# A fused sparse attention and FFN kernel: all engine orders from a list schedule, and the value product turned around

## Chip, cores and metric

One core of a Trainium2 chip. The metric is the device time of one execution in microseconds; lower is better. A profiled execution gives the span from the first to the last instruction, about 2 us shorter than the time. The profile names TensorE PE (its weight loads PEld), VectorE DVE, ScalarE ACT, GpSimd POOL and SyncE SP.

## The reference

```python
# q, k, v: (4, 8, 768, 64); sampled_blocks: (24, 3), blocks of 32
scores = q @ k.T / 8
mask = |block_i - block_j| <= 1, or first/last block row or column, or sampled
attn = softmax(where(mask, scores, -1e9));  x = attn @ v
x = x.transpose(0, 2, 1, 3).reshape(3072, 512)
out = (((x @ w1) * (x @ w2)) @ w3) @ w_out       # d_ff = 1024
```

Both kernels compute every score, take the exponential without a maximum, multiply by a 0/1 mask, and fold w3 @ w_out into one matrix first.

## The kernel before

The order on each engine is the order of the program text. A step makes two score tiles (`scores`), the values of the step before (`values`), and takes two pieces of weight or FFN work from a queue as filler (`pop`).

```python
def scores(b, t, Q, kp, i):
    s = ps_s.tile([128, 2, 512], F32, ...)                 # 2 buffers, 2 PSUM banks each
    for k2 in range(2):
        for h in range(2):                                 # two heads on the two row halves
            matmul(s[:, h, k2*256:(k2+1)*256], lhsT=kT[64*h:64*h+64, ...128 keys],
                   rhs=qT[64*h:64*h+64, ...256 queries])
    e = Exp(s / 8);  e = e * mask                          # ACT, then DVE
def values(b, t, Q, kp):                                   # output: features x tokens
    for k2 in range(2):
        for part in range(3):
            for g in range(4):                             # four heads on the four column quarters
                if part == 2: matmul(d[32*g:32*g+32], lhsT=ones, rhs=e)          # denominator
                else:         matmul(o[32*g:32*g+32, part], lhsT=v[..32 features], rhs=e)
def normalize(b, t, Q):
    ln = Ln(d);  rec = Exp(-ln)                            # ACT
    x[...] = o * rec                                       # DVE
...
transposes(0, 0); transposes(0, 1)
for t in range(NT): build_mask(t)                          # all masks before the first score
for s, g in enumerate(groups):
    scores(b, t, Q, kp, 0); scores(b, t, Q, kp, 1)
    if prev is not None: values(*prev); finish(prev)
    ...                                                    # transposes of the next batch
    pop(0 if s < 3 else 2)
    prev = g
```

## Time and profile before

| | before |
|---|---|
| time, median (range), first measurement | 300.67 us (299.7 to 305.25) |
| span of the profiled run | 298.6 us |
| busy PE / DVE / ACT | 272.0 / 194.2 / 189.5 us |
| first score, first value | 20.5, 23.7 us |
| granted TensorE clock, mean | 0.997 |

"Busy" counts a matmul from its start to its modelled end, so neighbours overlap and a busy TensorE can still lose time between pieces. The prediction shows how the pace is read from starts. The mean clock leaves out the start: the views give 1.00 there, though the eight score matmuls at 20.52 us take 1.04 us, against 0.61 later, which is half the pace.

### The profile page before, as it was taken

To read this page: it belongs to the slowest core of one execution; us is meant where nothing else is said; L and a number is where in the kernel's file an instruction comes from. 1 tells how busy PE (TensorE), PEld (TensorE's weight loads), DVE (VectorE), ACT (ScalarE), POOL (GpSimd) and SP (SyncE) were. 2 spreads that over 40 slices of the span, in tenths; PEclk is the share of its full clock that TensorE was granted. 3 is DMA by queue.
4 is the path that set the end of the run, shared out by engine and by line. 5 is a ranking of instruction groups with operands and counts; after the bars stand their busy time and mean duration, and the time that the engine had idled before them with its cause. 6 is when DMAs were issued, how large, how long until landed. Compare 5 with 4: busy or idle time off the path is not lost.

```text
span 298.6 us, 7850 instructions
## 1 busy us (share of the span) xinstructions
PE 272.0 (91%) x3412; PEld 141.2 (47%) x3412; DVE 194.2 (65%) x308; ACT 189.5 (63%) x250; POOL 49.6 (17%) x81
## 2 busy tenths in 40 slices
PE   0479888987999999999999999999999999999994
PEld 0335455555454455555455455555445445444441
DVE  3616787778767776776777677677767676643332
ACT  1088766656688886576867887657988778721310
POOL 8634487222200000332100000000000000000000
PEclk9999999999999999999999999999999999999998
DMA  7999999973420002757311000011000120003003
GB/s 96 150 204 207 206 173 186 180 106 55 66 44 2 0 2 108 131 69 106 55 37 73 35 2 2 2 72 70 3 2 1 52 93 2 0 2 140 0 12 129
DMA packets 20053, 21.46 MB, mean 72 GB/s; under 512 B 1588, under 2 KB 14900, under 8 KB 20020
## 3 DMA queue, kind: packets, MB, share of 16 engines
q0 software_dynamic: 16528, 14.68, 32.5%
q1 hardware_dynamic: 3492, 6.29, 5.6%
q8 instruction: 26, 0.43, 0.6%
q14 instruction: 7, 0.06, 0.1%
HBM read 29.36 MB, written 6.29 MB: 119 GB/s over the span
## 4 chain that ended last, share of the span: by engine, by line
PE 68%; ACT 15%; DVE 10%; issue 4%; POOL 1%; ACTq 0%; POOLq 0%
PE o L231 13%; PE pa L290 12%; PE pb L301 12%; ACT e L206 10%; PE po L311 10%; PE s L201 9%; PE wp L272 5%; DVE x L247 4%; PE d L228 4%; ACT rec L246 3%; PE tp L187 3%; DVE qkt L190 2%; ACT ln L244 2%; DVE e L207 1%; ACT mask L177 1%
## 5 line engine op out<-in xcount | busy, mean ns | idle before, releaser
L206 ACT ACTIVATE e<-s 128x1024 bf16<-128x1024 f32 x144 | 139.5, 1021 | 54.8 <-PE s L201 54.4
L207 DVE TENSOR_TENSOR e<-e,mask 128x1024 bf16<-128x1024 bf16 x144 | 99.1, 691 | 55.3 <-ACT e L206 55.3
L231 PE MATMUL o<-e,vn 128*32 128x256 bf16 x1152 | 54.8, 278 | 3.8 <-DVE x L247 1.8
L201 PE MATMUL s<-qkt 64*128 64x256 bf16 x576 | 47.5, 277 | 5.6 <-DVE qkt L190 3.9
L290 PE MATMUL pa<-x,w_sb 128*128 128x512 bf16 x192 | 49.7, 381 | 0.0
L301 PE MATMUL pb<-x,w_sb 128*128 128x512 bf16 x192 | 49.2, 379 | 0.0
L303 DVE TENSOR_TENSOR h<-pb,a 128x512 bf16<-128x512 f32 x48 | 33.1, 690 | 21.2 <-PE pb L301 21.2
L311 PE MATMUL po<-wf_sb,h 128*128 128x512 bf16 x192 | 44.5, 380 | 0.0
L293 ACT CAST a<-pa 128x512 bf16<-128x512 f32 x48 | 28.0, 583 | 26.1 <-PE pa L290 25.7
L228 PE MATMUL d<-e,ones 128*32 128x256 bf16 x576 | 42.4, 276 | 0.0
L201 PEld LDWEIGHTS <-qkt 64*128 64x128 bf16 x576 | 22.8, 95 | 37.5 <-issue 34.8
L231 PEld LDWEIGHTS <-vn 128*32 128x32 bf16 x1152 | 26.9, 96 | 20.5 <-issue 18.4
L301 PEld LDWEIGHTS <-w_sb 128*128 128x128 bf16 x192 | 18.7, 98 | 24.1 <-issue 2.6
L311 PEld LDWEIGHTS <-h 128*128 128x128 bf16 x192 | 17.5, 98 | 21.9 <-issue 2.7
L290 PEld LDWEIGHTS <-w_sb 128*128 128x128 bf16 x192 | 15.7, 98 | 21.1 <-issue 7.0
L316 DVE COPY ob<-po 128x512 f32<-128x512 f32 x24 | 16.5, 688 | 10.2 <-PE po L311 10.2
L85 POOL DMA_DIRECT2D qn<-in_q_dram x16 | 11.7, 728 | 66.7 <-PE tp L187 59.4
L247 DVE TENSOR_TENSOR x<-o,rec 128x512 bf16<-128x512 f32 x24 | 16.6, 692 | 1.6 <-ACT rec L246 0.9
L228 PEld LDWEIGHTS <-ones 128*32 128x32 bf16 x576 | 17.0, 98 | 0.4
L190 DVE COPY qkt<-tp 128x1536 bf16<-128x1536 bf16 x16 | 15.2, 950 | 1.3 <-PE tp L187 1.3
L272 PE MATMUL wp<-wo_sb,w3t_sb 128*128 128x512 bf16 x64 | 15.2, 380 | 0.0
L85 POOL DMA_DIRECT2D vn<-in_v_dram x16 | 11.6, 726 | 17.5 <-PE d L228 14.6
(54 smaller groups left out, 125.7 us busy)
## 6 DMA issues: line engine op xcount, KB each, us to landing
out_dram<-ob SPq DMA_DIRECT2D x24, 256.0 KB, 2.0
qn<-in_q_dram POOLq DMA_DIRECT2D x16, 192.0 KB, 4.2
kn<-in_k_dram POOLq DMA_DIRECT2D x16, 192.0 KB, 4.8
vn<-in_v_dram POOLq DMA_DIRECT2D x16, 192.0 KB, 5.8
w_sb<-in_moe_w_dram POOLq DMA_DIRECT2D x8, 256.0 KB, 10.6
w_sb<-in_moe_w_dram POOLq DMA_DIRECT2D x16, 128.0 KB, 5.3
wo_sb<-in_moe_w_out_dram POOLq DMA_DIRECT2D x1, 1024.0 KB, 11.3
rand_sb<-in_sampled_blocks_dram SPq DMA_DIRECT2D x1, 0.6 KB
```

The costliest lines, as they stand in the source:

```text
L201: nc.tensor.matmul(s[:, h, k2 * QT:(k2 + 1) * QT], lhsT=qk[64 * h:64 * h + 64, 1, kc * 128:(kc + 1) * 128], rhs=qk[64 * h:64 * h + 64, 0, ...
L206: nc.scalar.activation(e, s, AF.Exp, scale=1.0 / 8.0)
L207: nc.vector.tensor_tensor(e, e, mask[:, t, kp:kp + 1, :].to_broadcast((128, 2, 512)), op=ALU.mult)
L228: nc.tensor.matmul(d[rows, :], lhsT=ones, rhs=rhs, start=first, stop=last, skip_group_check=True)
L231: nc.tensor.matmul(o[rows, part * QT:(part + 1) * QT], lhsT=vn[b, 2 * Q + i][:, h, kc, 32 * part:32 * part + 32], rhs=rhs, start=first and ...
L247: nc.vector.tensor_tensor(X[i][:, 2 * Q:2 * Q + 2, half * QT:(half + 1) * QT], o.rearrange("p (s n) -> p s n", s=2), rec.to_broadcast((128 ...
L272: nc.tensor.matmul(box["p"], lhsT=w3t_sb[:, j, i * 128:(i + 1) * 128], rhs=wo_sb[:, j, :], start=j == 0, stop=j == NF - 1)
L290: nc.tensor.matmul(p, lhsT=w1_sb[:, c, f * 128:(f + 1) * 128], rhs=x[:, c, :], start=c == 0, stop=c == 3)
L293: nc.scalar.copy(a, p)
L301: nc.tensor.matmul(p, lhsT=w2_sb[:, c, f * 128:(f + 1) * 128], rhs=x[:, c, :], start=c == 0, stop=c == 3)
L303: nc.vector.tensor_tensor(hT[:, f, :], p, box["a"], op=ALU.mult)
L311: nc.tensor.matmul(box["o"], lhsT=hT[:, f, n * 128:(n + 1) * 128], rhs=wf_sb[:, f, :], start=f == 0, stop=f == NF - 1)
```

## The change

Intent: the number of TensorE columns falls, and so does the number of changes of array shape (from the full array to row halves or column quarters, and back). Every engine's order comes from a list schedule, a program that gives each free engine a ready task in turn; it runs at build time over a table of durations, buffers and a model of the DMA rings (the queues of transfers), instead of from the program text. The core:

```diff
+        for j, ...:                                       # tokens x features, full array
+            for k2 in range(2):
+                for qt in range(2):
+                    for h in range(2):
+                        nc.tensor.matmul(o[:, qt, h, :], lhsT=e[:, j, h, lo:lo + 128],
+                                         rhs=w[:, h, kc, :], ...)     # [v, 1]: 65 columns
+        rec = reciprocal(o[:, :, :, 64:]);  xn = o[:, :, :, :64] * rec          # DVE
+        nc.sync.dma_start(out=x[...], in_=xn[:, qt, :], transpose=True)         # 24 of them
-                        nc.tensor.matmul(d[rows, :], lhsT=ones, rhs=rhs, ...)
-                        nc.tensor.matmul(o[rows, ...], lhsT=vn[..., 32 columns], rhs=rhs, ...)
-        nc.scalar.activation(ln, d, AF.Ln);  nc.scalar.activation(rec, ln, AF.Exp, scale=-1.0)
-        nc.vector.tensor_tensor(e, e, mask)               # 144 of 1024 elements
+        nc.vector.tensor_tensor(e, e, mask)               # 72 of 2048 elements
+    # first q/k pair in halves by SP and ACT queues, cast on chip; 20 of 32 q/k and 2 of 8 w3
+    # transposes by DMA; w1, w2 in natural row order; 59 dummy matmuls on zeros at the start
+class Task:  # costs per engine, deps, buffers written and read, priority, array shape
+class Rings: # two DMA queues sharing the engines packet by packet; gives each landing time
+class Plan:
+    def run(self):
+        while ...:
+            # for each ready task: earliest start from deps (+ 0.05 to 0.195 us to be seen),
+            # free buffers and the engine; the earliest pick of all engines is committed
+    def pick_pe(self, cands, free, mode):
+        # stay in the score shape while scores are ready; enter it when both score buffers
+        # are (nearly) free; otherwise by priority
+log = plan.run()
+for t in log: t.go(t)                                     # the program text in that order
```

## The prediction

> **What bounds the kernel now.** I read the page's engine shares and 40 slices first, then the groups, then the timeline of a steady stretch, of the start and of the end. The time is 300.67 us, the profiled span 298.6 us, so I count in the span and take the time as up to 1% more.
>
> The page, engine shares and two rows of the slices:
>
> ```profile
> PE 272.0 (91%) x3412; PEld 141.2 (47%) x3412; DVE 194.2 (65%) x308; ACT 189.5 (63%) x250; POOL 49.6 (17%) x81
> ...
> PE   0479888987999999999999999999999999999994
> ...
> DMA  7999999973420002757311000011000120003003
> ```
>
> TensorE is the bound: after the first tenth it is nearly always busy, DVE and ACT are at two thirds. But busy is not peak, so I need its real pace. A steady step of the timeline (columns: start, duration, engine, line, operation):
>
> ```profile
> 146.40 0.61 PE L201 MATMUL s<-qkt 64*128 64x256 bf16 x8
> 146.83 1.94 ACT L206 ACTIVATE e<-s 128x1024 bf16<-128x1024 f32 x2 [0.61 <-PE s L201]
> 146.94 0.40 PE L231 MATMUL o<-e,vn 128*32 128x256 bf16 x8
> ...
> 147.71 1.04 PE L290 MATMUL pa<-x,w_sb 128*128 128x512 bf16 x4
> ...
> 148.58 1.03 PE L301 MATMUL pb<-x,w_sb 128*128 128x512 bf16 x4
> ...
> 149.54 0.61 PE L201 MATMUL s<-qkt 64*128 64x256 bf16 x8
> ```
>
> One step (two score tiles, their values, eight FFN matmuls) takes 149.54 - 146.40 = 3.14 us: scores 0.54, values and denominators 0.77, FFN 0.87 + 0.96. ACT works 1.94 us of exponentials and waits, so ACT is not the limit. Two more rows give the pace of back-to-back matmuls, the first from 285 us on, the second from 53 us on:
>
> ```profile
> 287.46 7.07 PE L311 MATMUL po<-wf_sb,h 128*128 128x512 bf16 x32
> ...
> 55.17 0.62 PE L259 MATMUL w3p<-ident,w_sb 128*128 128x128 bf16 x8
> ```
>
> With one matmul's own 0.38 and 0.22 us taken off, a 512-column matmul takes (7.07 - 0.38)/31 = 0.216 us, a 128-column one with its weight load (0.62 - 0.22)/7 = 0.057 us. The line through both is 0.0045 us + 0.000413 us per column: estimates of 0.110 us for 256 columns and 0.031 us for 65. The step then has 4 x 0.110 (score matmuls run in pairs of row halves) + 6 x 0.110 (values in fours of column quarters) + 8 x 0.216 = 2.83 us of streaming; the other 0.31 us lies at its three changes of array shape, about 0.10 us each. Over the kernel:
>
> - streaming: scores 31.7 (288 slots), values with denominators 47.5 (432 slots), FFN 124.4 (576), weight fold 13.8 (64), q/k transposes 11.0 (192 slots), w3 transposes 3.7, masks 2.3; sum 234.4 us
> - shape changes in 72 steps: 72 x 0.31 = 22.3 us
> - the start: scores begin at 20.5 us with about 3.8 us of TensorE work before them, so 16.7 us are lost
> - the end: last matmul at about 294.5 us, then copy and store, 4.1 us
> - the rest, 298.6 - 277.5 = 21.1 us: transposes wedged into 16 steps, half-speed matmuls and waits for exponentials around 20 to 30 us, single waits, and the FFN tail
>
> The start and end:
>
> ```profile
> 10.60 0.59 PE L167 MATMUL gp<-hot,Ab 24*24 24x512 bf16 x1 [10.60 <-DVE Ab L161]
> ...
> 12.26 0.85 PE L187 MATMUL tp<-ident,qn 128*64 128x128 bf16 x12
> ...
> 20.52 1.04 PE L201 MATMUL s<-qkt 64*128 64x256 bf16 x8
> ...
> 294.56 0.69 DVE L316 COPY ob<-po 128x512 f32<-128x512 f32 x1 [1.04 <-PE po L311]
> ```
>
> q and k are long there when their transposes run: the fixed order puts a mask product first, which waits 10.6 us for a chain of small DVE instructions, then all nine mask tiles stand ahead of the first score.
>
> **What the Trainium skill says.** "TensorEngine Tiling (Array Packing)", Key Properties: "Mode switching requires drain". The trace agrees: 0.10 us at each change. The same page, Restrictions and Gotchas, says that column tiling excludes Fast Weight Load; today's values use it (32-column weights), the new ones don't. "TensorE: Matmul & The Clock Gate", Weight-path perf modes, gives a theoretical 32 cycles for a 128-column weight load that reads four ways, and the section on the back-to-back gap about 25 ns as the floor of any matmul. Together they allow 0.031 us for a 65-column matmul that loads 128 new columns each time; the trace only shows that such a load fits into 0.057 us. "DMA: Bandwidth & Descriptors", DMA Transpose (X-bar), allows transposes of 2-byte data from the hardware queues; no run of the kernel before has one.
>
> **The change part by part.** The counts are those of the built kernel's instruction order.
>
> 1. Values with the exponentials stationary and [v, 1] moving: 1152 matmuls of 65 columns on the full array in place of 1728 of 256 columns four at a time. The denominator is the 65th column. 1152 x 0.031 = 36.1 against 47.5: -11.4 us. Ln and the exponential that made the reciprocal leave ACT (19.4 us busy); 48 small reciprocals come to DVE.
> 2. Transposes: the output is now tokens by features, so x needs 24 DMA transposes; 20 of the 32 q/k and 2 of the 8 w3 transposes go to DMA too. TensorE keeps 72 slots of q/k (4.1) and 48 of w3 (2.8): -7.8 us with their own switches and waits still to count.
> 3. Streaming of the FFN and fold stays (124.8 and 13.8; some 256-column pieces), scores 31.7, masks 2.3. Sum after: 215.6 us, -18.8.
> 4. Shape changes: values are now in the full-array shape, so only scores (75 blocks in the order, two sides each) and four column-tiled transposes change it: about 158 x 0.10 = 16 us, -6 us.
> 5. The start: q and k of the first pair come in halves by hardware queues, uncast, at 0.75 us. With the 2.0 us that a store takes to land here as a guide, then a cast, transposes and a copy, the first score is at about 6 us; masks and other transposes follow it. Lost: about 5.5 us plus 1 us at half clock, -10 us. Dummy matmuls keep the clock up in between.
> 6. The end: the last 512 columns leave in pieces of 256, 128 and 128: 3.4 us, -0.7.
> 7. The rest. 215.6 + 16 + 6.5 + 3.4 = 241.5 us without any wait. The order was made for few waits, but it is fixed, and where a duration in the table is off TensorE waits in order. I choose 3 us, against 21 before: TensorE's only filler while ACT is behind is now chosen tile by tile. Sum 244.5, and 245 us as time.
>
> Masks: 72 of 2048 elements in place of 144 of 1024 (0.691 us each). By the trace's 0.415 us for a 512-element and 0.950 us for a 1536-element 16-bit copy, 1024 more elements cost 0.53: 72 x 1.22 = 88 us, -11. It lies beside TensorE. DVE gains 24 normalizations' worth in 48 halves, 43 rearranging or widening copies (about 0.35 each, 15 us): near 187 us in all. ACT: 144 exponentials at 0.92 us apart = 132 us, 56 copies for the FFN 24, 20 output copies 10, others about 7: near 173 us by pace.
>
> **The rivals.**
>
> - The weight load doesn't hide. If each pair takes the 0.057 us of the 128-column case, the values take 66 us, +30: about 275 us. For it: the trace has no shorter pair with 128 columns of weights. Against it: the shape is the main point of the change, its table counts 0.24 us for eight (a claim, not a measurement here), and nothing shows 0.057 us to be the load's and not the 128 columns' time. I give it one in fourteen.
> - ACT or DVE takes over. The order has 47.6 us of FFN after the last value, so all exponentials fall between 6 and about 193 us: ACT then carries about 158 us of 187 (85%), DVE about 172 busy (92%, less by pace). With two score buffers and one output accumulator, a late exponential or mask stops TensorE. Against it: the average step is 2.55 us on TensorE, 2.2 on ACT, 2.4 at most on DVE. If DVE does bound the stretch I expect +5 to +12: 250 to 257 us.
> - DMA comes late. The slices show the queues full until about 60 us while attention now runs a fifth faster, and 46 transposes are added. A late x starves TensorE of filler and moves FFN work behind attention: +3 to +10.
> - The start or waits are better than I take them: 237 to 240 us, since 241.5 has no wait but my 0.10 us per change may be high in places.
>
> **Range and chances.** Only a slow weight load plus another failure reaches 295 us, so a same or slower result needs a cause that I don't see. From the rivals: 245, 237 to 257 holds it 8 times in 10; faster 0.97, same 0.02, slower 0.01.
>
> **What would show it.** Steps 1 and 3: the values' row in blocks of 8 at 0.25 us apart; twice that is the first rival. Step 4: scores to values and back still cost 0.1 us each, FFN to values none. Step 5: the first score at 6 us; beyond 9 the start is wrong. Step 7: PE at 9 in all slices but the first and the last, and few waits for the exponential or mask rows; gaps of 0.3 us and more in each step would mean ACT or DVE has become the bound; waits for the transposed x in the middle, the DMA. A time over 260 would make the sum wrong and not only its waits.

## The result

| | before | after |
|---|---|---|
| time, median (range) | 300.19 us (299.59 to 305.25) | 246.06 us (246.03 to 246.15) |
| ratio of fast runs | | 0.82 (0.8186 to 0.8215) |
| span | 298.6 us | 244.3 us |
| busy PE / DVE / ACT | 272.0 / 194.2 / 189.5 us | 239.1 / 174.5 / 184.9 us |
| first score, first value | 20.5, 23.7 us | 6.3, 18.8 us |

A ratio is the mean time of one kernel's fast runs over that of the other's fast runs of the same rounds, so it is not quite the ratio of the medians. Executions over 1.5% slower than the fastest of the same kernel are left out of the means. The 305.25 us of the kernel before is 1.9% above its fastest, so it is not among the fast runs.

The page of the changed kernel, engine shares and rows of the slices:

```profile
PE 239.1 (98%) x2659; PEld 136.5 (56%) x2659; DVE 174.5 (71%) x323; ACT 184.9 (76%) x238; POOL 48.2 (20%) x78
...
PE   7999999999999999999999999999999999999995
...
PEclk9999999999999999999999999999999999999999
DMA  7999999999727943699479779990034121300312
```

TensorE is full in every slice but the first and the last, and its clock is full from 5 us on (before that, see step 5 below). The DMA engines are far busier than before in the middle. A steady stretch of its timeline, TensorE's rows with ACT's exponentials:

```profile
120.69 0.61 PE L639 MATMUL s<-qkt 64*128 64x256 bf16 x8
121.13 1.94 ACT L645 ACTIVATE e<-s 128x1024 bf16<-128x1024 f32 x2 [0.44 <-PE s L639]
121.24 0.41 PE L662 MATMUL o<-v,e 128*128 128x65 bf16 x8
121.49 1.46 PE L745 MATMUL f<-x,w 128*128 128x512 bf16 x6
122.88 0.63 PE L639 MATMUL s<-qkt 64*128 64x256 bf16 x8
...
123.44 0.91 PE L662 MATMUL o<-v,e 128*128 128x65 bf16 x24
124.19 1.46 PE L745 MATMUL f<-x,w 128*128 128x512 bf16 x6
```

Scores to values still costs 121.24 - 120.69 - 0.44 = 0.11 us; values to FFN nothing: 8 x 0.031 = 0.25 us, and 121.24 + 0.25 is where the FFN starts. The 24 values give the pace: (0.91 - 0.19)/23 = 0.031 us, with one value's own 0.19 us taken off. The start and the end:

```profile
6.27 0.39 PE L639 MATMUL s<-qkt 64*128 64x256 bf16 x4 [0.37 <-DVE qkt L343]
...
18.80 0.90 PE L662 MATMUL o<-v,e 128*128 128x65 bf16 x24
...
237.62 3.66 PE L771 MATMUL f<-wf,big 128*128 128x512 bf16 x32
...
241.31 0.29 DVE L343 COPY ob<-f 128x128 f32<-128x128 f32 x1 [0.16 <-PE f L771]
```

And busy time in stretches of 40 us (columns: stretch, its length, then PE, PEld, DVE, ACT, POOL, clock, DMA share, GB/s):

```profile
60.00:100.00 40.00, 40.00 (x486) 22.44 (x484) 32.99 (x60) 34.78 (x43) 5.49 (x8) 1.00 0.65 105
100.00:140.00 40.00, 40.00 (x497) 21.67 (x494) 33.72 (x61) 36.21 (x45) 10.91 (x16) 1.00 0.89 139
```

ACT is at 87 to 91% and DVE at 82 to 84% there: near, but TensorE has no gap. The two spans by the same terms (streaming as the sums of the prediction; start is the first score less the TensorE work before it; the rest is what is left):

| us | before | predicted after | after |
|---|---|---|---|
| streaming at full pace | 234.4 | 215.6 | 215.6 (0.031 and 0.216 us confirmed) |
| changes of array shape | 22.3 | 16 | 16 to 17 (0.10 to 0.11 us each) |
| start | 16.7 | 5.5 + 1 | about 5.8 (first score at 6.3) |
| end | 4.1 | 3.4 | 3.0 (244.3 - 241.3) |
| the rest: waits, dummies, half clock | 21.1 | 3 | about 3 to 4 |
| span | 298.6 | 244.5 | 244.3 |

### The profile page after: what moved, and what is told of

Same layout as the page of the kernel before. It is cut to its first block, busy times and chain, and to the rows that moved or that the text cites. A ratio compares the mean times of both kernels' runs of the same rounds, so it can differ in the third digit from the quotient of the medians.

```text
span 244.3 us, 6361 instructions
## 1 busy us (share of the span) xinstructions
PE 239.1 (98%) x2659; PEld 136.5 (56%) x2659; DVE 174.5 (71%) x323; ACT 184.9 (76%) x238; POOL 48.2 (20%) x78
## 4 chain that ended last, share of the span: by engine, by line
PE 89%; DMA 5%; DVE 3%; issue 1%; ACT 1%; SPq 0%; POOL 0%; POOLq 0%
PE f L745 32%; PE f L771 17%; PE s L639 15%; PE o L662 14%; PE f L725 6%; DMA kn<-in_k_dram 4%; DMA rand_sb<-in_sampled_blocks_dram 1%; DVE e L649 1%; PE o L479 1%; PE f L585 1%; PE f L713 1%; PE f L529 1%; ACT e L645 0%; SPq L401 0%; ACT qkt L343 0%
## 5 line engine op out<-in xcount | busy, mean ns | idle before, releaser
L645 ACT ACTIVATE e<-s 128x1024 bf16<-128x1024 f32 x144 | 141.3, 1032 | 14.3 <-PE s L639 13.7
L745 PE MATMUL f<-x,w 128*128 128x512 bf16 (+1 forms) x448 | 94.5, 349 | 0.0
L649 DVE TENSOR_TENSOR e<-e,mask 128x2048 bf16<-128x2048 bf16 x72 | 87.2, 1214 | 8.8 <-ACT e L645 8.5
L756 DVE TENSOR_TENSOR big<-f,a 128x512 bf16<-128x512 f32 (+1 forms) x56 | 34.0, 609 | 37.5 <-PE f L745 28.2
L745 PEld LDWEIGHTS <-w 128*128 128x128 bf16 x448 | 39.1, 98 | 32.2 <-issue 5.1
L662 PEld LDWEIGHTS <-e 128*128 128x128 bf16 x1152 | 43.4, 97 | 16.6 <-DVE xn L675 3.8
L662 PE MATMUL o<-v,e 128*128 128x65 bf16 x1152 | 48.4, 194 | 0.3 <-DVE e L649 0.3
L753 ACT CAST a<-f 128x512 bf16<-128x512 f32 (+1 forms) x56 | 29.7, 532 | 23.5 <-PE f L745 23.5
L771 PE MATMUL f<-wf,big 128*128 128x512 bf16 (+2 forms) x208 | 47.3, 363 | 0.0
L639 PEld LDWEIGHTS <-qkt 64*128 64x128 bf16 x576 | 22.3, 94 | 27.3 <-issue 24.4
L771 PEld LDWEIGHTS <-big 128*128 128x128 bf16 x208 | 17.6, 98 | 17.1 <-issue 2.3
L675 DVE TENSOR_TENSOR xn<-o,rec 128x256 bf16<-128x256 f32 x48 | 20.1, 419 | 0.6
L379 POOL DMA_DIRECT2D kn<-in_k_dram x15 | 10.8, 722 | 3.5 <-issue 1.0
```

The source lines that it names most:

```text
L379: t = add(name, {POOL: 0.73}, lambda t: nc.gpsimd.dma_start(out=out_of(), in_=src), deps=deps, writes=writes, kind="load", prio=seq[0])
L639: nc.tensor.matmul(s[:, h, k2 * QT:(k2 + 1) * QT], lhsT=z[64 * h:64 * h + 64, 1, kc * 128:(kc + 1) * 128], rhs=z[64 * h:64 * h + 64, 0, t3 ...
L645: exps.append(add(f"E {m} {j}", {ACT: 0.915}, lambda t, sk=sk, ek=ek, j=j: nc.scalar.activation(T(*ek)[:, j], T(*sk), AF.Exp, scale=1.0 / ...
L649: tm = add(f"K {m}", {DVE: 1.137}, lambda t, ek=ek, t3=t3, kp=kp: nc.vector.tensor_tensor(T(*ek), T(*ek), mask[:, t3, kp:kp + 2, :].unsque ...
L662: nc.tensor.matmul(o[:, qt, h, :], lhsT=e[:, j, h, lo:lo + 128], rhs=w[:, h, kc, :], start=kc == 0 and qt == 0 and h == 0, stop=kc == C - ...
L675: tx = add(f"xn {rk}", {DVE: 0.342}, lambda t, rk=rk, ok=ok, xk=xk, pr=pr: nc.vector.tensor_tensor(T(*xk)[:, :, 128 * pr:128 * pr + 128].r ...
```

## The experiments

Three questions stay open after the traces: what the new arithmetic would be worth without the new order; whether TensorE's columns, weight loads and shape changes really are the bound everywhere; and what the order owes to its table and to the ring model. Twelve runs in three groups of four in the order of the table, each in three rounds beside the kernel before. The medians of the kernel before were 300.34, 300.33 and 300.43 us in the three groups, so they may be compared across them. The medians are over all executions; a_nospare, u_flat, a_k16 and a_trb2 have one slow execution each, which the ratios leave out, and the differences below are those of fast runs.

| run | time, median | ratio (95%) |
|---|---|---|
| b_values | 291.72 us | 0.9709 (0.9684 to 0.9735) |
| b_start | 296.53 us | 0.9876 (0.9852 to 0.9899) |
| a_v33 | 242.60 us, wrong on purpose | 0.8077 (0.8054 to 0.8099) |
| a_s4 | 262.76 us | 0.8739 (0.8713 to 0.8765) |
| after0 | 246.37 us | 0.8205 (0.8182 to 0.8227) |
| b_late | 286.62 us | 0.9541 (0.9518 to 0.9564) |
| a_nospare | 249.40 us | 0.8271 (0.8212 to 0.8329) |
| a_trb16 | 257.12 us | 0.8556 (0.8531 to 0.8581) |
| u_rings | 246.21 us | 0.8206 (0.8174 to 0.8238) |
| u_flat | 270.72 us | 0.9011 (0.8981 to 0.9042) |
| a_k16 | 252.96 us | 0.8420 (0.8399 to 0.8441) |
| a_trb2 | 269.13 us | 0.8945 (0.8911 to 0.8979) |

**b_values: the new value product in the old order.**

```diff
 # kernel before; values() and normalize() as in the change, w1 and w2 loaded in natural order
-    ln = Ln(d);  rec = Exp(-ln);  x = o * rec
+    rec = reciprocal(o[..., 64:]);  xn = o[..., :64] * rec;  x = DMA transpose of xn
```

> The kernel before, in its old fixed order, with the new value product alone (exponentials stationary, [v, 1] moving, reciprocal on DVE, x turned by DMA transposes). Theory: TensorE is the bound there too, so the values' streaming falls by 11.4 us and the change of shape between values and FFN goes (72 x 0.10 = 7 us): about 281 us, a step of 2.87 us instead of 3.14. Rival: in the old order of two score tiles and two fills per step, DVE or ACT takes the place of TensorE and the gain is under 8 us (293 us or more).

8.6 us less, between the two theories. Its timeline shows both at once:

```profile
145.69 0.61 PE L207 MATMUL s<-qkt 64*128 64x256 bf16 x8
146.24 0.66 PE L230 MATMUL o<-v,e 128*128 128x65 bf16 x16
146.73 1.89 PE L315 MATMUL po<-wf_sb,h 128*128 128x512 bf16 x8
148.56 0.61 PE L207 MATMUL s<-qkt 64*128 64x256 bf16 x8
149.40 0.97 PE L230 MATMUL o<-v,e 128*128 128x65 bf16 x16 [0.23 <-DVE xn L248]
```

The step from 145.69 to 148.56 takes the expected 2.87 us. In the next one the first value stands 0.84 us after the scores instead of 0.55: it waits for the normalization that frees the accumulator. So the arithmetic is worth what was computed, but not at the ends of units.

**b_late: the same, with the filler moved in between.**

```diff
-        if prev is not None: values(*prev); finish(prev)
         ...
         pop(0 if s < 3 else 2)
+        if prev is not None: values(*prev); finish(prev)
```

> b_values with one move: in each step the two pieces of filler go between the scores and the values instead of after the values. Theory: the new values alone gave 8.6 us and not 19 because the next unit's first value waits for the normalization that frees the two accumulators (0.5 us and more at each of 24 unit ends, about 13 us of waits for it); with filler in between the wait is hidden: 278 to 283 us. Rival: the loss is the DVE's additional work, then nothing changes: 290 us or more.

5.1 us less again, all by moving the same instructions; the direction is shown, the size was expected at 9 to 14. In its list of waits those for the normalization have left the top, and another has come: TensorE's transposes wait for exponentials to free a score buffer.

```profile
PE tp L185 <- ACT e L212: 11.3, 14, 0.9
```

The order by hand cures one wait and makes another. The new arithmetic gives 13.7 us in the best old order that I tried, of the whole change's 54.

**b_start: an early start alone.**

```diff
     transposes(0, 0); transposes(0, 1)
+    four score tiles and their exponentials, masked later
     for t in range(NT): build_mask(t)
```

> The kernel before with only its start changed: transposes of the first two pairs and four score tiles go ahead of the mask work. Theory: time won at the start is won at the end, since TensorE is full afterwards: first score near 8.5 us instead of 20.5, but the masks still cost about as much, so 5 to 8 us less, about 294 us. Rival: the loads of weights bound the first 60 us anyway, and the gain is under 2 us.

3.8 us less: neither. The first score came at 8.95 us, 11.6 us earlier, but ACT then copied the nine masks from 14.3 to 19.9 us, and the first value came here:

```profile
19.22 0.62 PE L225 MATMUL o<-e,vn 128*32 128x256 bf16 x8
```

That is 4.5 us earlier than the 23.7 us of the kernel before, and nearly the gain. This one case fits the reading that in the old order the first *value* was the event that counted; it does not show it. In the changed kernel it comes at 18.8 us, hardly earlier than in b_start, but by then TensorE has done transposes, masks and eight score tiles, against four here: more of the time in front of it is used.

**a_v33: half the moving columns.**

```diff
-                            matmul(o[:, qt, h, :], ..., rhs=w[:, h, kc, :], ...)
+                            c0 = 0 if kc == 0 else 32
+                            matmul(o[:, qt, h, c0:], ..., rhs=w[:, h, kc, c0:], ...)
```

> The changed kernel with 33 instead of 65 moving columns in 960 of the 1152 value matmuls (wrong result on purpose). If the columns set the pace, the line of 0.0045 us + 0.000413 us per column gives 0.018 us each, 960 x 0.013 = 12.5 us less TensorE time, of which ACT at about 90% may give back some: 236 to 240 us. If the load of the 128 stationary columns or a floor per matmul sets it, the pace stays at 0.030 us and the time at 246 us.

The time fell by 3.8 us against after0, a third of what columns alone would give. One block of 33-column values in its timeline:

```profile
149.32 0.36 PE L663 MATMUL o<-v,e 128*128 128x33 bf16 x8
```

With one matmul's own 0.178 us taken off that is (0.36 - 0.178)/7 = 0.026 us each, against 0.031 with 65 columns; 960 x 0.005 = 4.8 us, of which 3.8 appear in the time. So half the columns take only a sixth off the pace: a floor, of the weight load or of the matmul itself (the run does not tell which), lies not far under the 65 columns. Fewer than 33 were not tried. My line through 128 and 512 columns happened to hold at 65 and fails at 33.

**a_s4: more changes of array shape.**

```diff
-            if s:                                         # stay in the score shape
+            if s and all(c[1].mode == "S" for c in soon): # leave it when anything else is ready
-        if s and (not rest or self.feed(s, free)):
+        if s and (not rest or (mode != "S" and self.feed(s, free))):
```

> The changed kernel with score tiles one at a time where other work is ready: 138 blocks of score matmuls instead of 75, the same work. Theory: each change of array shape costs 0.10 us of TensorE and TensorE is the bound: 63 x 2 x 0.10 = 12.6 us more, 258 us. Rival: the drains fall into waits that are there anyway: under 4 us more.

16.4 us more than after0 for 63 more blocks, 0.26 us a block or 0.13 a side. Its timeline, one score tile between FFN pieces:

```profile
121.58 0.39 PE L639 MATMUL s<-qkt 64*128 64x256 bf16 x4
121.90 0.60 PE L745 MATMUL f<-x,w 128*128 128x512 bf16 x2
```

121.90 - 121.58 - 2 x 0.110 = 0.10 us, the drain as in the kernel before. The drains account for 12.6 us; the remaining 4 fit the idle time of TensorE in its trace (37.7 us busy of 40 from 140 to 180 us), though that profile is of its slowest execution (265.78 us, with a granted clock of 0.83 in the first 20 us and 0.96 from 140 to 180), so this part is not shown.

**after0 and a_nospare: the dummies.**

```diff
-    return Task("spare", ..., lambda t: nc.tensor.matmul(... zero ...), "spare", 0, mode)
+    return Task("spare", ..., lambda t: None, "spare", 0, mode)
```

> The changed kernel again, unchanged, as the measure for the other runs on this chip: 246 us, ratio 0.82.

> The changed kernel without its 59 dummy matmuls, all else in the same order. Theory: without them TensorE starts at half clock[...]: 1 to 3 us more. Rival: the early phase waits for copies and masks anyway: under 0.5 us.

after0 repeats the result. Without dummies the fast runs were 246.39, 248.85 and 249.95 us, against 245.99 to 246.92: up to 3 us more, and far less even. The interval of the ratio overlaps with that of after0, so the mean gain is not shown. In the one trace, of the fastest run, two score tiles at 8.38 us still go at half pace (8 matmuls in 1.04 us, 0.61 at full clock), and from 14 to 16 us its granted clock is at 0.50 again. So the dummies do raise the clock, but whether that is worth the expected 1 to 3 us or the rival's 0.5 is not decided.

**a_trb16: all q/k transposes on TensorE.**

```diff
-           aprio=0.0, ..., trb=6,
+           aprio=0.0, ..., trb=16,
```

> The changed kernel with all q/k transposes on TensorE (10 more pairs, 9 of them column-tiled), newly scheduled. Theory: TensorE is the bound everywhere, so 120 slots x 0.057 = 6.9 us and 18 blocks x 2 changes x 0.10 = 3.6 us come on top: 256 us. Rival: the DMA transposes hold something up, and without them the time stays or falls.

257.12 us, 10.8 more than after0, where 10.5 were expected: TensorE is the bound, and work given to it adds up nearly one for one. (Counted in the traces, the changes of shape rise by 28 and not 36, as some transposes stand next to scores; the same sum then gives 9.7.) It also prices the DMA transposes of q and k in the shipped kernel at about 11 us.

**u_rings and u_flat: the ring model.**

```diff
+        if t.kind == "load": t.slack, t.least = 0.0, t.end + 5.0
-        self.rings.push(queue, t.end + 1.5, t.packets, t.each, t)
+        self.rings.push(queue, t.end + 1.5, t.packets, 0.001 if t.kind == "load" else t.each, t)
```

> Control for the next run: the changed kernel with two more buffers each for w3/h rows and for transposed w3, newly scheduled with the ring model as it is. Both theories: within 1 us of 246 us.

> The same buffers, but the schedule takes every load from GpSimd to land 5 us after its issue, whatever else is in flight (no ring model for loads; the trace has medians from 5.8 to 14.4 us). Theory: the order puts work on weights and q/k/v too early in the first 60 us, and TensorE, which runs in order, waits for them: 4 us or more above the control. Rival: semaphores take up the difference and TensorE has other work: under 1.5 us.

The control is at 246.21 us, the fast runs of u_flat at 270.56 (median): 24.4 us for the modelled landing times alone, far over the 4 that I had set as the least. Rows of u_flat, the clock slices of its page and busy time in stretches, and what TensorE waited for, and two blocks of six transposes after and long after such a wait:

```profile
PEclk9988878965999999999999999999999999999999
...
20.00:40.00 20.00, 13.60 (x133) 6.95 (x132) 11.80 (x22) 8.99 (x11) 8.81 (x14) 0.84 1.21 204
40.00:60.00 20.00, 14.63 (x190) 9.13 (x188) 11.31 (x25) 12.87 (x16) 3.39 (x5) 0.84 1.30 178
...
PE o L664 <- DVE e L651: 6.0, 3, 3.7
PE f L587 <- ACT qs L345: 2.6, 1, 2.6
...
PE f L715 <- DMA big<-in_moe_w_dram: 2.0, 1, 2.0
...
39.01 0.82 PE L587 MATMUL f<-ident,qs 128*128 128x128 bf16 x6 [2.62 <-ACT qs L345]
...
43.70 0.50 PE L587 MATMUL f<-ident,qs 128*128 128x128 bf16 x6
```

From 20 to 60 us TensorE is busy for 28 us of 40, and its granted clock is at 0.84, so the work that is there slows down too. (The Trainium skill, "TensorE: Matmul & The Clock Gate", HAM oscillation, warns of idle gaps of more than about 3.4 us. Here shorter ones were enough: after 2.62 us the six transposes at 39.01 go at about half pace, and no wait before it was longer.) Waits for loads run through ACT and DVE: one q tile came late, ACT waited 4.0 us for it, and TensorE for ACT; for another, DVE waited 4.4 us, and the longest wait of TensorE, 3.7 us, is for the mask product behind it. I had not counted the clock.

**a_k16: a wrong entry in the table.**

```diff
-        tm = add(f"K {m}", {DVE: 1.137}, ...)
+        tm = add(f"K {m}", {DVE: 1.6}, ...)
```

> The changed kernel scheduled with a wrong table: the mask multiplication counted at 1.6 us, where the trace has 1.21 us. Theory: a fixed order is only as good as its table, but a too long DVE time makes the order cautious rather than wrong; TensorE stays full: 1 to 4 us more. Rival: the table's exactness is what removes the waits: over 6 us more.

Its fast runs took 252.77 to 252.96 us (the profile fell in a slow one and is not used): 6.6 us more than after0 from one duration that is 0.4 us too long. That is the rival's size: a too long entry costs too. By which waits is not shown, as the only trace is of the slow execution; and one wrong entry in one direction is one case. Against the rival that any other order than the tuned one costs as much stands u_rings: its order on TensorE differs as well (503 matmuls from 60 to 100 us against 486), and its time does not.

**a_trb2: an attempt to do better.**

```diff
-           ..., trb=6,
+           ..., trb=2,
```

> An attempt to beat the changed kernel: only two q/k pairs are transposed on TensorE, the other 14 by DMA. If TensorE is all that counts, 24 + 6 slots x 0.057 = 1.7 us and two changes less: 244 us. Rival: the rings are full in the first 60 us, as the slices show, so earlier DMA transposes come late and the first score and mask phase waits: 248 us or more.

268.79 us in the fast runs (median): 22.4 us worse. TensorE's longest wait (us in total, times, longest) and its stretches around it:

```profile
PE s L639 <- DMA qkt<-qs: 10.0, 1, 10.0
...
34.00:38.00 4.00, 3.20 (x20) 1.43 (x18) 0.76 (x2) 1.05 (x2) 1.95 (x3) 1.00 1.20 192
38.00:42.00 4.00, 0.00 (x0) 0.00 (x0) 0.36 (x1) 0.12 (x1) 1.23 (x2) 0.73 1.27 192
42.00:46.00 4.00, 0.00 (x0) 0.00 (x0) 1.09 (x3) 0.00 (x0) 2.26 (x4) 0.50 1.28 191
46.00:50.00 4.00, 1.65 (x12) 0.86 (x13) 0.00 (x0) 1.84 (x3) 1.52 (x3) 0.50 1.24 195
50.00:54.00 4.00, 3.53 (x40) 2.16 (x40) 2.99 (x4) 3.60 (x5) 0.00 (x0) 0.56 1.22 194
```

A single wait of 10.0 us for a transposed q or k, while the rings are full (DMA share 1.2 to 1.3). The clock stays up for the first microseconds of the wait, then falls to half and stays there until about 53 us, so the work after the wait (from 47.5 us) pays as well. With six pairs on TensorE the kernel has no such wait. The schedule's own model had foreseen this wait: when the recorded kernels are built again without the chip, printing when each task is planned to end, the plan of a_trb2 holds a gap of about 10 us before that score tile and ends at 264.5 us. The shipped plan ends at 239.5 (measured span 244.3), a_trb16's at 250.8 (255.4), u_rings' at 239.5 (244.7), and u_flat's, with its false landing times, at 239.3 (268.8): the plan is itself a forecast, good where its times are.

Without a run: score tiles in 16 bits in PSUM (the memory that matmuls write), to make blocks of four tiles and halve the shape changes, did not build; six exponential buffers instead of four give the identical order on all engines; by my notes, several other values of the schedule's parameters end with no task able to start. The reverse of b_values, the list schedule over the old arithmetic, was not run, so no experiment splits the 54 us between arithmetic and order.

## Why the prediction was right

**Steps 1 and 3, streaming.** Right, with the pace at 0.031 us as estimated. The first rival, a weight load that doesn't hide, is refuted by the trace. That the estimate held is partly luck: a_v33 shows that the line fails at 33 columns.

**Step 2, DMA transposes.** Right for TensorE as far as q and k go (a_trb16: 10.8 us for ten pairs); the transposes of x and w3 have no run of their own. The rival that DMA comes late is real in a_trb2 and u_flat, and the shipped order avoids it.

**Step 4, shape changes.** Right: 0.10 to 0.11 us each in the trace, 0.13 a change in a_s4 with whatever else its order brings. The trace has the 75 score blocks that were counted; it has one column-tiled block where four were counted, and some changes for masks that were not.

**Step 5, the start.** The lost time is as predicted (first score at 6.3 us for 6), in part by luck: the first q and k took 3.3 to 3.6 us to land, not the 2.0 us taken as a guide. Of the 1 us added for half clock 0.3 appeared: the six transposes from 4.39 to 5.03 us go 0.107 us apart instead of 0.057. What was not seen is that an early score alone is worth little (b_start: 3.8 us for 11.6); it is worth its time only if the order fills the gap.

**Step 6, the end.** 3.0 us for 3.4.

**Step 7, the rest.** Right in size, 3 to 4 us for 3, and the boldest choice: it carries about 17 of the 54 us, as what the other terms leave, not as the result of an experiment. I chose it because TensorE's filler is picked tile by tile; b_values and b_late show the waits that an order by hand leaves, u_flat and a_k16 that time is lost again with wrong times in the table. The place of the rest was not seen: 25 of the dummies, 256 columns each, stand between 9.4 and 19 us and fill 25 x 0.110 = 2.75 us of it, while from 20 to 140 us TensorE has no gap. ACT was near its limit as read (busy for 88% of the time from 6.3 to 193 us); DVE was put too high, at 187 us busy for 174.5, and is at 84% there. In the step read first, ACT also has a cast of 0.59 us beside its 1.94 us of exponentials; it still waits, so the conclusion holds.

The sum agrees more closely (244.5 for 244.3 us) than its terms, whose small errors cancel.

## What to carry to other kernels

When one engine is the bound, add its work up from start-to-start paces, plus shape changes, start and end; what is left is waits, and that term can be as large as the saving in streaming (about 17 us here against 18.8). New arithmetic dropped into an old order collects only part of its worth, because it moves the waits: look at what frees the accumulators. A fixed order needs true durations and above all true landing times of DMA: waits of 2 us and more on a bound TensorE were paid twice here, as idle time and as a lower clock.

## What the Trainium skill lacked or had wrong

- "TensorEngine Tiling (Array Packing)", Key Properties, says that a mode switch drains TensorE, without a figure: 0.10 to 0.11 us at each change between the row-halved score matmuls and the others, 16 us of this kernel.
- "TensorE: Matmul & The Clock Gate", Back-to-back issue gap, gives sustained 81 ns at 128 columns and 131 ns at 512 for pairs of weight load and matmul; here they take 57 ns and 216 ns. The formula that the same section keeps for an isolated matmul, columns over 2.4 plus 2.5 ns, is the one that fits these pairs: 56 and 216 ns, and an estimate of 30 ns for 65 columns, where the trace has 31. The page's formula for a weight load (LDWEIGHTS), columns over 1.2 (107 ns for 128), is not the pace here: pairs with 128 new weight columns run at 31 ns with 65 moving columns and 26 ns with 33, close to the 25 ns floor that the page gives for a matmul.
- The same page, HAM oscillation, warns of a lower clock after idle gaps of more than about 3.4 us. a_trb2 agrees: after 10.0 us of waiting it runs at 0.50 for some 6 us more. But the limit is not a safe one: u_flat falls to half clock after waits of 2.0 and 2.6 us, and a_nospare is at 0.50 from 14 to 16 us with no wait over 0.3 us since its first matmul.
- "DMA: Bandwidth & Descriptors", DMA Transpose (X-bar), has no latency for a transpose beside other traffic: from issue to landing a median of 3.8 us (x), 4.4 us (q, k) and 14.1 us (w3, while weights load) in the changed kernel.
